# Two interleaved attention and squared-ReLU layers on one core: sums and biases off GpSimd, output bias written into the accumulator banks, own buffers for the first token pair, the full chunk first

## The chip, the cores and the metric

One core of a Trainium2 chip runs the whole program. The metric is the device time of one execution in microseconds (us); of several runs the median counts.

## The reference

Two layers, each a linear attention block (A) and a dense block (B), on 2048 tokens of 640 columns in float32:

```
x = x + A(layernorm(x));  x = x + B(layernorm(x));  and both once more, with the same weights
A: q, k, v = x @ wqkv  (32 heads of 20);  phi(t) = where(t > 0, t + 1, exp(t)) + 1e-6
   kv = sum over tokens of phi(k) (x) v;  z = sum over tokens of phi(k)
   o = phi(q) @ kv / (phi(q) . z + 1e-6);  A = o @ wo
B: h = relu(x @ w1 + b1);  B = (h * h) @ w2 + b2      (w1: 640 x 1728, w2: 1728 x 640)
```

## The kernel before

The 2048 tokens are 16 tiles of 128 (`t`), and four tiles make a group of 512 tokens (`g`). Each float32 operand of a matmul is split into a high part, rounded to the format fp32r, and a low part, the rest: a copy on ScalarE makes the high part, a subtraction on VectorE the low part, and a product is three matmuls (high x low, low x high, high x high).

Each layer has two stages. The **attention stage** goes over the 16 tiles with an order written out by hand. It makes `phi(k)` and `phi(q)`, stores `phi(q)` in DRAM (`pqd`), and sums up the products from which `kv` is made; `phi(q)` of some tiles is made late, at the end of the stage (`late_q`), and the last such piece within the next stage (`late_line`). In layer 0 the stage also splits the weights of B and keeps the halves in DRAM (`Prep`, lines 409 to 475); pairs of 128-row chunks of w1 are turned into the four sums and differences of a Strassen scheme (`Prep.sums`, four additions on GpSimd). Then `kv` and `wo` are multiplied into one matrix M, and tiles 0 to 3 get the attention output and become x1.

The **second stage** is ordered by a planner that runs while the program is built: `Clock` (line 80 on) keeps a time for each engine, and a set of generators (`Line`s, each with a rank; the lower goes first) give their next step with an estimated cost. `Clock.run` puts TensorE's steps one after the other and fills the other engines' queues up to TensorE's time. The instructions stand in each engine's queue in the order in which the planner took them, and every engine works its queue in order. A step may be of kind `"any"`: then the planner puts it on the engine that ends it first. The lines are:

- `fc1_line`: the first layer of B, for each group 14 chunks of hidden units. `STEPS` gives their order: chunk 13 (64 units, both halves of its weights side by side in one matmul, 10 matmuls), chunk 12 (15 matmuls), then six Strassen steps of two chunks each (`Strassen.seg1` to `seg5`, matmuls at line 1497 and 1507). Chunk 12 goes into bank `h`, chunk 13 into bank `h1`; the Strassen steps use both.
- `act` (line 1576): what follows each chunk. For a full chunk: ReLU with bias on ScalarE (line 1585), the square rounded on ScalarE (1598), the square in full on VectorE or GpSimd (1599), the low part on VectorE (1588). For chunk 13 five shorter steps (1618, 1604, 1608, 1591, 1592).
- `fc2_line`: the second layer of B. For each chunk, in the order in which they were made, its product with w2 (`fc2_tile`, line 1646) is added into five banks: `a0` to `a3`, one for each tile with 512 output columns, and `as`, the other 128 columns turned, for all four tiles. The first chunk of a group (`FIRST` = 13) starts the sums in a bank, and after the last (`LAST` = 11) VectorE adds the bank to x1 (`tile_add`, line 1695; the turned strip goes by block moves, line 1672).
- For tiles 4 to 15, in pairs: `q_line` loads and turns `phi(q)` (line 766) and splits it (`p_split`); `pair_line` makes the sums of the Strassen scheme (`s_turns`, line 1747, VectorE or GpSimd), splits them into `so`, and does seven products (`Pair`, matmuls at line 567, all into bank `po0`, additions at line 1813); `x_line` does the layer norm, turns the tile (lines 542 to 555) and splits it into the group's buffer `xTb`, and then `bias` adds b2 to x1 on GpSimd (`f_bias`, line 835) and stores it. `t_line` makes the first-layer sums (`t_sums`, line 1337) and splits them into `tx`. A pair's `q_line` starts when the pair before is turned (`("turned", t - 2)`), and its split waits for the products of the pair before (`("p", ...)`).
- `bias_line` does the same `bias` for tiles 0 to 3; `late_line` the last late `phi(q)`; `ring_line` loads B's weights into a ring of buffers in the order of `uses` (line 367; the load is at line 496), each as soon as a buffer is free. All loads and stores of this stage go through SyncE's queue, in order.

Of the kernel before, what the change touches and what calls it, by code (L numbers as in the profile page):

```python
# [13 lines left out]
P = 128  # L14
# [3 lines left out]
DC = D // P  # L18
# [22 lines left out]
STEPS = (("p", 13), ("p", 12), *(("w", i) for i in range(NW)))  # L41
FIRST, LAST = 13, 11
# [37 lines left out]
class Clock:  # L80
# [22 lines left out]
    def head(self, line):  # L103


        while not line.over:
# [26 lines left out]
            elif h[0] == "end f":  # L133
                self.f += [line.got - HOP if len(h) > 2 else line.ready - HOP] * h[1]
# [91 lines left out]
def kernel(  # L226
# [39 lines left out]
    b2bc = cpool.tile([P, D], F32, name="b2bc")  # L266
    b1sb = cpool.tile([P, NF], F32, name="b1sb")
# [100 lines left out]
    for g in range(NG):  # L368
        for kind, c in STEPS:
# [4 lines left out]
            else:  # L374
                q = (13, 12) if c == 0 else (2 * c - 2, 2 * c - 1)
# [33 lines left out]
    class Prep:  # L409


        def __init__(self):
# [7 lines left out]
            self.pair, self.summed = {}, set()  # L420
# [19 lines left out]
        def sums(self, c):  # L440

            r0, r1 = self.pair[c]
# [9 lines left out]
        def high(self):  # L452
            if self.raws:
                nm, c, raw = self.raws.pop(0)
                while nm in ("wG", "wH") and c not in self.summed:
                    self.low()
                u = utile("uprep")[:, : unit_len(nm, c)]
# [164 lines left out]
    for layer in range(N_LAYERS):  # L622
# [209 lines left out]
        def f_bias(t):  # L832

            v = xr.pop(t)
            nc.gpsimd.tensor_tensor(out=v, in0=v, in1=b2bc, op=ALU.add)
            yield
            nc.sync.dma_start(x1d[t], v)

# [52 lines left out]
        for t in range(NT):  # L891
# [173 lines left out]
            for _ in range(4):  # L1065
                prep.low()
            if gt and not is_late:
# [257 lines left out]
        def t_sums(t, eng):  # L1325
# [5 lines left out]
            for out, x, y in (  # L1331
# [5 lines left out]
                eng[0].tensor_tensor(out=out, in0=x, in1=y, op=ALU.subtract)  # L1337
# [42 lines left out]
        for i in (2, 3):  # L1380
# [10 lines left out]
        list(t_sums(0, [nc.gpsimd]))  # L1391
# [5 lines left out]
        list(t_sums(2, [nc.vector]))  # L1397
# [4 lines left out]
        ta, tb, so = wtile("uT13"), wtile("uT42"), wtile("uS")  # L1402
        ta, tb, so = (
            ta.rearrange("p (j m n) -> p j m n", j=2, m=2),
            tb.rearrange("p (j m n) -> p j m n", j=2, m=2),
            so.rearrange("p (j n) -> p j n", j=2),
# [30 lines left out]
        x1_first, pT_first = [x1_tile()], [pT_tile()]  # L1437

# [9 lines left out]
        def fc1(g, c):  # L1448
            ps = fresh("h" if c == 12 else "h1")
# [101 lines left out]
        def both(cols, f):  # L1551
            eng = {"DVE": nc.vector, "POOL": nc.gpsimd}
            return "any", [(e, cost(e, cols)) for e in eng], lambda e: f(eng[e])

# [3 lines left out]
        def stepped(it, eng, cols):  # L1558
            def f(e):
                eng[0] = e  # L1560
                next(it)

            return both(cols, f)

        slots = {"h": [0.0] * 3, "hr": [0.0] * 3}

# [9 lines left out]
        def act(c, ps, at):  # L1576
# [19 lines left out]
            def full():  # L1596
                yield "ready", there
                yield "ACT", cost("ACT", GT), lambda: nc.scalar.activation(h[:, 0], r, AF.Square)  # L1598
                yield both(GT, lambda e: e.tensor_tensor(out=r, in0=r, in1=r, op=ALU.mult))  # L1599
# [3 lines left out]
            def half():  # L1603
# [3 lines left out]
                free[1] = line.ready  # L1607
# [9 lines left out]
            else:  # L1617
                at = ck.chain("ACT", cost("ACT", GT), lambda: nc.scalar.activation(
                    r[:FL], ps[FL:], AF.Identity, bias=b1sb[FL:, 13:14]
                ), at)  # L1620
                line = ck.add(half(), 0, at)
# [4 lines left out]
        def fc2_tile(g, c, h, i, s=slice(0, DM), new=False):  # L1626
# [3 lines left out]
            first, last = c == FIRST, c == LAST  # L1630
# [4 lines left out]
            ps = accs[g, i]  # L1635
            if i < TG:
# [8 lines left out]
            for k, (l, r) in enumerate(a):  # L1645
                nc.tensor.matmul(  # L1646
                    ps, l, r, start=(first or new) and k == 0, stop=end and k == len(a) - 1
                )

# [85 lines left out]
        def s_turns(t, eng):  # L1735


            z0, z1 = yzp.pop(t), yzp.pop(t + 1)
            a, b, r = slice(0, 2 * P), slice(2 * P, 4 * P), slice(4 * P, D)
            for out, x, y, op in (  # L1740
# [6 lines left out]
                eng[0].tensor_tensor(out=out, in0=x, in1=y, op=op)  # L1747
# [9 lines left out]
        def p_split(t, first=0):  # L1757

            u = pT_first.pop() if pT_first else pT_tile()
# [19 lines left out]
        class Pair:  # L1779
# [21 lines left out]
            def turned(self, c):  # L1801
# [466 lines left out]
```

## Time and profile before

| | |
|---|---|
| median of 3 runs | 1389.21 us (1384.1 to 1390.07) |
| the profiled execution | 1390.24 us, span 1388.4 us |
| TensorE busy | 1337.4 us, 96% |
| VectorE / ScalarE / GpSimd busy | 1014.8 / 744.8 / 235.1 us |
| mean granted TensorE clock | 0.990 |
| additions of b2 on GpSimd | 32, 54.2 us |

In the rows a line begins with the line of the code, the engine (PE is TensorE, DVE VectorE, ACT ScalarE, POOL GpSimd, SPq SyncE's queue of DMA issues), the operation, and what it writes and reads with its shape. In a timeline the first two numbers are start and length in us, and a bracket gives the idle time before and what ended it. In a wait row three numbers follow: us in total, how often, the longest. Groups have a count, then busy us and mean ns. A row of stretches has the stretch, its length, busy us and instructions of the five engines, the granted clock, the DMA engines' busy share and GB/s. The attention stage of layer 0 ends at about 260 us, layer 1's second stage begins at about 947 us.

### The profile page before, as it was taken

What the parts mean: (1) busy time and instruction counts of PE and PEld (TensorE: products, weight loads), DVE (VectorE), ACT (ScalarE), POOL (GpSimd) and SP (SyncE); (2) the same over time, 40 slices, a digit from 0 to 9 for tenths busy, and PEclk for the clock granted to TensorE, in tenths of its full rate; (3) what the DMA queues carried; (4) which work ended last, traced back from release to release, by engine and by line L of the source; (5) the groups of instructions that cost most, each with busy time, mean ns of one, the idle gap of its engine ahead of it and who ended that gap; (6) DMA issues with size and microseconds to landing.
All of it is one profiled execution on the core that took longest, in us unless ns stands there. A gap on an engine that the chain in (4) does not pass through costs nothing.

```text
span 1388.4 us, 21426 instructions
## 1 busy us (share of the span) xinstructions
PE 1337.4 (96%) x7616; PEld 1184.3 (85%) x7616; DVE 1014.8 (73%) x1883; ACT 744.8 (54%) x1724; POOL 235.1 (17%) x264
## 2 busy tenths in 40 slices
PE   9999999889989999999999999998999999999999
PEld 8888889778877988988888889997887888888887
DVE  8888968879768778755256778788788877875323
ACT  5888845635545444536436777564255445454321
POOL 2334310301102001100012232103012111020000
PEclk9999999999999999999999999999999999999999
DMA  6678686397787688699741114264976977687685
GB/s 199 223 267 328 246 273 191 124 320 248 243 258 248 235 264 294 216 366 346 259 155 57 58 39 122 53 200 161 354 245 213 308 243 261 203 291 268 235 316 175
DMA packets 120096, 316.10 MB, mean 228 GB/s; under 512 B 14966, under 2 KB 40182, under 8 KB 119318
## 3 DMA queue, kind: packets, MB, share of 16 engines
q1 hardware_dynamic: 118478, 312.06, 66.1%
q10 hardware_dynamic: 1512, 2.69, 0.7%
q8 instruction: 60, 0.98, 0.3%
q14 instruction: 46, 0.38, 0.1%
HBM read 251.28 MB, written 64.85 MB: 228 GB/s over the span
## 4 chain that ended last, share of the span: by engine, by line
PE 55%; DVE 19%; DMA 13%; ACT 5%; issue 3%; SPq 3%; POOL 1%; ACTq 0%; DVEq 0%; POOLq 0%
PE PS L567 21%; PE PS L1646 17%; PE PS L1497 12%; DMA pqt<-pq 5%; PE PS L1507 3%; ACT z L555 2%; DMA u<-kept_w 2%; SPq L766 1%; DMA u<-kept_wH 1%; PE PS L1463 1%; DVE e L678 1%; DMA u<-kept_wF 1%; DVE bn L517 1%; DVE z L553 1%; DVE uprep L404 1%
## 5 line engine op out<-in xcount | busy, mean ns | idle before, releaser
L1646 PE MATMUL PS<-u,h 128*128 128x512 f32 x1318 | 342.0, 395 | 8.9 <-DVE h L1592 6.5
L555 ACT ACTIVATE z<-y 32x160 f32<-32x160 f32 x781 | 261.1, 334 | 57.8 <-DVE y L542 37.6
L1646 PEld LDWEIGHTS PS<-u,h 128*128 128x128 f32 x1318 | 242.6, 191 | 55.6 <-DVE h L1592 7.3
L567 PE MATMUL PS<-kq,xT 128*128 128x320 f32 (+2 forms) x1575 | 283.6, 335 | 2.5 <-DVE r L679 2.2
L567 PEld LDWEIGHTS PS<-kq,xT 128*128 128x128 f32 x1575 | 251.3, 189 | 28.5 <-DVE r L679 2.5
L1497 PE MATMUL PS<-tx,u 128*128 128x256 f32 x1152 | 162.7, 284 | 8.5 <-DMA u<-kept_wH 3.7
L1585 ACT ACTIVATE hr<-PS,b1sb 128x512 f32<-128x512 f32 x104 | 71.3, 686 | 173.6 <-PE PS L1507 156.8
L1497 PEld LDWEIGHTS PS<-tx,u 128*128 128x128 f32 x1152 | 150.7, 192 | 15.2 <-ACT s L1519 5.2
L1497 PEld LDWEIGHTS PS<-xTb,u 128*128 128x128 f32 x864 | 120.9, 192 | 24.6 <-DVE PS L1539 6.8
L1497 PE MATMUL PS<-xTb,u 128*128 128x256 f32 x864 | 129.4, 286 | 9.8 <-DVE PS L1539 4.4
L567 PE MATMUL PS<-kh,xh 128*128 128x512 f32 x480 | 126.8, 398 | 0.0
L1599 DVE TENSOR_TENSOR hr<-hr 128x512 f32<-128x512 f32 x98 | 68.0, 700 | 76.9 <-ACT h L1598 76.5
L522 POOL TENSOR_SCALAR rs<-mv 128x1 f32<-128x1 f32 x62 | 29.1, 470 | 544.4 <-DVE mv L519 537.8
L567 PEld LDWEIGHTS PS<-kh,xh 128*128 128x128 f32 x480 | 88.9, 192 | 15.2
L1598 ACT ACTIVATE h<-hr 128x512 fp32r<-128x512 f32 x104 | 64.6, 628 | 61.9 <-PE PS L1646 60.4
L670 ACT ACTIVATE e<-PS 128x320 f32<-128x320 f32 (+4 forms) x128 | 53.2, 434 | 81.8 <-PE PS L567 68.6
L1646 PE MATMUL PS<-h,u 128*128 128x512 f32 x328 | 92.6, 391 | 0.0
L678 DVE TENSOR_SCALAR e<-e 128x320 f32<-128x320 f32 (+4 forms) x128 | 49.7, 388 | 47.6 <-ACT e L670 46.9
L1588 DVE TENSOR_TENSOR h<-hr,h 128x512 fp32r<-128x512 f32 x104 | 75.9, 735 | 3.4
L854 POOL TENSOR_TENSOR acc<-acc,r 128x640 f32<-128x640 f32 x28 | 51.2, 1829 | 156.5 <-DVE r L679 156.5
L1507 PE MATMUL PS<-xTb,u 128*128 128x512 f32 x288 | 76.8, 393 | 0.0
L1646 PEld LDWEIGHTS PS<-h,u 128*128 128x128 f32 x328 | 59.9, 188 | 11.0
(173 smaller groups left out, 1949.5 us busy)
## 6 DMA issues: line engine op xcount, KB each, us to landing
u<-kept_w SPq DMA_DIRECT2D x116, 640.0 KB, 5.8
u<-kept_wE SPq DMA_DIRECT2D x48, 512.0 KB, 4.9
u<-kept_wH SPq DMA_DIRECT2D x48, 512.0 KB, 5.5
u<-kept_wG SPq DMA_DIRECT2D x48, 512.0 KB, 5.4
u<-kept_wF SPq DMA_DIRECT2D x48, 512.0 KB, 5.7
x<-x SPq DMA_DIRECT2D x48, 320.0 KB, 6.0
pqt<-pq SPq DMA_DIRECT2D x128, 80.0 KB, 5.8
x<-xr SPq DMA_DIRECT2D x32, 320.0 KB, 6.3
```

The lines of the kernel that those rows point to most:

```text
L555: nc.scalar.activation(d, v, AF.Copy)
L567: nc.tensor.matmul(ps, a, b, start=first and i == 0, stop=last and i == 2)
L670: nc.scalar.activation(self.e[:, a:b], ps, AF.Exp)
L678: nc.vector.tensor_scalar(e, e, 1.0, PHI_EPS, op0=ALU.min, op1=ALU.add)
L854: nc.gpsimd.tensor_tensor(out=acc, in0=acc, in1=r, op=ALU.add)
L1497: nc.tensor.matmul(ps, l[:, d], r[:, d], start=start and d == 0 and n == 0, stop=d == 1 and n == 2, skip_group_check=True,)
L1507: nc.tensor.matmul(ps, l[:, k], r, start=False, stop=n == 2, skip_group_check=True)
L1585: nc.scalar.activation(r, ps, AF.Relu, bias=b1sb[:, c : c + 1])
L1588: nc.vector.tensor_tensor(out=h[:, 1], in0=r, in1=h[:, 0].bitcast(F32), op=ALU.subtract)
L1598: yield "ACT", cost("ACT", GT), lambda: nc.scalar.activation(h[:, 0], r, AF.Square)
L1599: yield both(GT, lambda e: e.tensor_tensor(out=r, in0=r, in1=r, op=ALU.mult))
L1646: nc.tensor.matmul(ps, l, r, start=(first or new) and k == 0, stop=end and k == len(a) - 1)
```

## The change

- **Full chunk first.** In group 0 of each layer chunk 12 goes ahead of chunk 13, and chunk 13 is put into bank `po0` there. The order of the weight loads follows. In the other groups the order stays, and a Strassen step waits in the plan until chunk 13's bank is read.
- **Sums.** `s_turns` and `t_sums` are on VectorE alone. The full square of a chunk may go to VectorE or ScalarE. `Prep.sums` stays on GpSimd but is issued later, behind the tile's other GpSimd work.
- **Output bias.** For tiles 0 to 3 the addition of b2 to x1 goes from GpSimd to VectorE. For groups 1 to 3 it is gone: ScalarE writes b2 into each accumulator bank (`preset`) after the bank has been read, and the group's first matmul adds to it; x1 is stored as soon as it is there (`x1_keep`). A second copy of b2's last 128 values, one per partition, is loaded for that.
- **Own buffers.** The first pair (tiles 4 and 5) keeps its split operands in the buffer that group 1's `xTb` takes later (`early`). The second pair's `q_line` starts after the first pair's `q_line`, and waits no longer for the first pair's products; `x_line` of group 1 waits until the first pair is done.
- `late_line` goes from rank 4 to 1, and the first sums of group 0 wait for it in the plan.

The diff, cut; the names behind `#` say where a line stands.

```diff
-STEPS = (("p", 13), ("p", 12), *(("w", i) for i in range(NW)))
-FIRST, LAST = 13, 11
+UNITS = tuple(("w", i) for i in range(NW))
+STEPS = ((("p", 12), ("p", 13), *UNITS), *(NG - 1) * ((("p", 13), ("p", 12), *UNITS),))
+LAST = 11
...
+        nc.sync.dma_start(b2col, b2[DM:].rearrange("(p o) -> p o", o=1))
...
-                q = (13, 12) if c == 0 else (2 * c - 2, 2 * c - 1)
+                q = (12, 13) if (g, c) == (0, 0) else (13, 12) if c == 0 else (2 * c - 2, 2 * c - 1)
...
                 if nm == "wF":
-                    self.sums(c)
-                    self.summed.add(c)
+                    self.to_sum = c
...
-            nc.gpsimd.tensor_tensor(out=v, in0=v, in1=b2bc, op=ALU.add)
+            nc.vector.tensor_tensor(out=v, in0=v, in1=b2bc, op=ALU.add)
...
+        def x1_keep(t):
+            nc.sync.dma_start(x1d[t], xr[t])
...
             for _ in range(4):
                 prep.low()
+            prep.sums()
...
-                eng[0].tensor_tensor(out=out, in0=x, in1=y, op=ALU.subtract)      # t_sums
+                nc.vector.tensor_tensor(out=out, in0=x, in1=y, op=ALU.subtract)
...
+        early = tmp.tile([P, 2 * DC * GT], R32, tag="T", name="early", bufs=2)
+        so_of = {TG: early[:, 4 * D : 6 * D + 8 * P].rearrange("p (j n) -> p j n", j=2)}
...
-            ps = fresh("h" if c == 12 else "h1")
+            ps = fresh("h" if c == 12 else "h1" if g else "po0")
...
+            def square(e):
+                if e == "ACT":
+                    nc.scalar.activation(r, r, AF.Square)
+                else:
+                    nc.vector.tensor_tensor(out=r, in0=r, in1=r, op=ALU.mult)
...
-                yield both(GT, lambda e: e.tensor_tensor(out=r, in0=r, in1=r, op=ALU.mult))
+                yield "any", [(e, cost(e, GT)) for e in ("DVE", "ACT")], square
...
+        def preset(g, i):
+            accs[g, i] = ps = fresh(f"a{i}" if i < TG else "as")
+            if i < TG:
+                nc.scalar.activation(ps, b2bc[:, :DM], AF.Copy)
+            else:
+                nc.scalar.activation(ps, b2col.to_broadcast([P, GT]), AF.Copy)
...
-                eng[0].tensor_tensor(out=out, in0=x, in1=y, op=op)                 # s_turns
+                nc.vector.tensor_tensor(out=out, in0=x, in1=y, op=op)
...
-            u = pT_first.pop() if pT_first else pT_tile()                          # p_split
+            if t < TG + 2:
+                k = t - TG
+                u = early[:, 2 * k * D : 2 * (k + 1) * D].rearrange("p (j n) -> p j n", j=2)
+            else:
+                u = pT_first.pop() if pT_first else pT_tile()
...
-            yield "need", ("p", (t - 2) // 2 * 2)                                  # q_line
+            if t > TG + 3:
+                yield "need", ("p", (t - 2) // 2 * 2)
...
+            yield "need", ("p", t - 2)                                             # pair_line, after the turns
...
+            yield "SP", MB, store                                                  # x_line: x1_keep
...
-            yield "need", ("group", t // TG - 1)                                   # x_line
+            yield "need", ("group", t // TG - 1), ("p", TG)
...
-            yield from bias(t)                                                     # end of x_line
...
+                    yield "until", lambda: not half_of                             # fc1_line, before seg1
...
+                        if g < NG - 1:
+                            ck.add(preset_line(g + 1, i), 2, free["a", i])         # after tile_add
...
-            after = ("turned", t - 2)
+            after = ("q", t - 1) if t == TG + 2 else ("turned", t - 2)
...
-        ck.add(late_line(), 4, 7.5)
+        ck.add(late_line(), 1, 7.5)
```

More of the change, by code (lines that the diff above doesn't have):

```diff
@@ L1629, in fc2_tile @@
             wh, wl = u[:, :D], u[:, D:]
-            first, last = c == FIRST, c == LAST
+            first, last = (g, i) not in accs, c == LAST
             end = last or last_layer and (g, i, c) == (NG - 1, TG - 1, 9)
@@ L1646, in fc2_tile @@
                 nc.tensor.matmul(
[L1647 removed]
+                    ps, l, r, start=(first or new) and k == 0, stop=end and k == len(a) - 1, **loose
                 )
+        def preset(g, i):
[4 more added lines that the diff above has]
+                nc.scalar.activation(ps, b2col.to_broadcast([P, GT]), AF.Copy)
         strips = {}
@@ L1871 @@
         ck.t["ACT"], ck.t["DVE"] = 4.5, 4.8
-        free = {0: 0.0, 1: 0.0, **{("a", i): 0.0 for i in range(TG + 1)}}
+        free = {0: 0.0, 1: 0.0, 2: 0.0, **{("a", i): 0.0 for i in range(TG + 1)}}
         done = ck.done
@@ L1981, in bias @@
             it = f_bias(t)
-            yield "POOL", cost("POOL", D), lambda: next(it)
+            yield "DVE", cost("DVE", D), lambda: next(it)
             def store():
@@ L2138, in fc1_line @@
                         yield "until", room
-                        turned(g, c, fresh("h1" if k else "h"), k)
+                        turned(g, c, fresh(("h", "h1", "po0")[k]), k)
                         continue
@@ L2168, in fc1_line, with preset_line, f @@
                     turned(g, 2 * c + 1, st.h1, 1)
+        def preset_line(g, i):
+            line = ck.lines[-1]
+            def f():
+                preset(g, i)
+            yield "ACT", cost("ACT", DM), f
+            free["a", i] = line.ready
         def fc2_line():
```

79 lines of the change are left out of this document (46 added, 33 removed).

## The prediction

> **What bounds the kernel now.** I read the page's busy times first, then the waits of TensorE, then the timeline where those waits lie, then the clock there.
>
> ```profile
> span 1388.4 us, 21426 instructions
> PE 1337.4 (96%) x7616; PEld 1184.3 (85%) x7616; DVE 1014.8 (73%) x1883; ACT 744.8 (54%) x1724; POOL 235.1 (17%) x264
> ...
> PE PS L567 <- DVE xr L1813: 7.9, 6, 2.8
> PE PS L1646 <- DVE h L1592: 6.5, 3, 3.5
> ...
> PE PS L1463 <- DVE xTb L1777: 3.7, 2, 2.2
> ```
>
> TensorE works in all but 51.0 us (1388.4 - 1337.4), and the change takes no matmul away. So whatever it brings must come out of those 51.0 us, or out of the time that matmuls lose to a lowered clock. A wait row gives the total, the number of times and the longest: a few long waits, nearly all on VectorE. The three on L1592 (the low half of hidden chunk 13, the 64-row chunk with which each group opens) are 1.49 us at the start of each layer's group 0 and 3.52 us at layer 0's step from group 0 to 1. Layer 0's group 0 starts so:
>
> ```profile
> 261.81 5.96 PE L1463 MATMUL PS<-xTb,u 128*128 128x512 f32 x25 [0.63 <-ACT xTb L283]
> ...
> 268.76 0.98 PE L1497 MATMUL PS<-xTb,u 128*128 128x256 f32 x6 [0.99 <-DVE hr L1604]
> ...
> 272.79 7.18 POOL L835 TENSOR_TENSOR xr<-xr,b2bc 128x640 f32<-128x640 f32 x4
> 273.07 1.57 DVE L1591 CAST h<-hr 64x512 fp32r<-64x512 f32 x1
> ...
> 274.68 1.92 DVE L1592 TENSOR_TENSOR h<-hr,h 64x512 fp32r<-64x512 f32 x1
> ...
> 276.65 1.19 PE L1646 MATMUL PS<-u,h 128*128 128x512 f32 x4 [1.49 <-DVE h L1592]
> ...
> 278.95 0.98 PE L1497 MATMUL PS<-xTb,u 128*128 128x256 f32 x6 [1.11 <-DVE PS L1539]
> ...
> 280.70 0.32 SPq L2087 DMA_DIRECT2D pq<-rl  x1
> ...
> 283.81 0.38 SPq L496 DMA_DIRECT2D u<-kept_wH  x1
> ...
> 288.59 0.98 PE L1497 MATMUL PS<-tx,u 128*128 128x256 f32 x6 [1.80 <-DMA u<-kept_wH]
> ...
> 290.17 4.47 PE L1646 MATMUL PS<-u,h 128*128 128x512 f32 x12 [0.60 <-DMA u<-kept_w]
> ```
>
> Four bias additions hold GpSimd from 272.79 to 279.97, and in that time VectorE's steps for chunk 13 take 1.57 and 1.92 us; at the next group, beside no bias, the same two take 0.41 and 0.69 (rows below). So TensorE waits 1.49 and 1.11 us there. The 0.99 us before are for bank h1, which chunk 13 and the first product of the Strassen steps share. The two waits for weights follow from SyncE's queue: the load of wH stands at 283.81 behind the store of the late `phi(q)` row, issued at 280.70.
>
> ```profile
> 288.00:292.00 4.00, 2.81 (x10) 2.27 (x11) 3.90 (x8) 2.09 (x5) 0.00 (x0) 0.74 1.00 372
> 292.00:296.00 4.00, 4.00 (x19) 3.15 (x18) 0.90 (x3) 0.71 (x2) 0.00 (x0) 0.84 1.03 419
> ...
> 394.00:398.00 4.00, 2.94 (x10) 2.46 (x11) 3.93 (x8) 1.80 (x5) 0.00 (x0) 0.71 0.11 46
> 398.00:402.00 4.00, 4.00 (x24) 3.72 (x24) 1.81 (x6) 0.75 (x2) 0.00 (x0) 0.86 0.81 306
> ...
> 972.00:980.00 8.00, 5.76 (x21) 4.62 (x22) 5.79 (x11) 2.43 (x5) 0.00 (x0) 0.79 1.02 386
> ```
>
> The third column from the right is the granted clock. After the waits it falls: 4 x 0.26 + 4 x 0.16 = 1.68 us lost at 288 to 296, 4 x 0.29 + 4 x 0.14 = 1.72 at 394 to 402, 8 x 0.21 = 1.68 in layer 1. These are counted as busy, so waits cost more than the idle time says.
>
> **The change, part by part.** *Start of group 0 (full chunk first, chunk 13 in bank po0, biases and late row).* Chunk 12 now goes first and chunk 13 into a bank of its own, so the 0.99 us go. The four biases move to VectorE, where each is one 640-column addition, 0.81 us by the row of L1813 below, four 3.2 us in all; they are queued at rank 6, behind the hidden chunks, so I cost them at nothing. Without that cover they cost TensorE the 1.11 us that it waits for VectorE now. The 1.49 and 1.11 us go. Sum: 0.99 + 1.49 + 1.11 = 3.59 us a layer. The waits for weights (1.80 + 0.60 = 2.40) and the lost clock (1.68) go if the late row is stored before it blocks SyncE, for which the change raises its rank. But the DMA engines are full there (shares 1.00 and 1.03), so I count half: (2.40 + 1.68) / 2 = 2.04. Against this stands a new wait: the weights of w2 chunk 12 go to the buffer that the first chunk's 15 matmuls free.
>
> ```profile
> u<-kept_w SPq DMA_DIRECT2D x116, 640.0 KB, 5.8
> ```
>
> They end at 261.81 + 5.96 x 15/25 = 265.4, and a load lands 5.8 us later, at 271.2. TensorE could use it from about 269.5 (25 matmuls, then the first products). The planner in the code reckons a landing of 3.7 us (1.3 + 0.655/0.39 + 0.7), so it may place this work 2.1 us too early: between 0 and 2.1, I take 1.5, since its error is one-sided. Net: 3.59 + 2.04 - 1.5 = 4.1 a layer, 8.3 for two.
>
> *Group 0 to group 1 (own buffers for the first token pair).*
>
> ```profile
> 300.80 1.85 SPq L766 DMA_DIRECT2D pqt<-pq  x4
> ...
> 324.13 0.49 DVE L1813 TENSOR_TENSOR xr<-PS,xr 128x320 f32<-128x320 f32 x1
> ...
> 337.65 1.04 PE L567 MATMUL PS<-uM,pT 128*128 128x320 f32 x6
> ...
> 385.58 5.96 PE L1463 MATMUL PS<-xTb,u 128*128 128x512 f32 x25 [1.52 <-DVE xTb L1777]
> ...
> 393.87 0.41 DVE L1591 CAST h<-hr 64x512 fp32r<-64x512 f32 x1
> 394.32 0.69 DVE L1592 TENSOR_TENSOR h<-hr,h 64x512 fp32r<-64x512 f32 x1
> ...
> 395.06 2.41 PE L1646 MATMUL PS<-u,h 128*128 128x512 f32 x6 [3.52 <-DVE h L1592]
> ...
> 1065.49 5.96 PE L1463 MATMUL PS<-xTb,u 128*128 128x512 f32 x25 [2.20 <-DVE xTb L1777]
> ```
>
> Group 1 starts late because its tokens are late: tile 6's `phi(q)` is loaded only when tiles 4 and 5 are turned (300.80), its split waits for the first pair's last product (324.13), so the second pair starts at 337.65, 13.5 us after the first ended. Meanwhile group 0's work runs out, and nothing is left to lay beside the opening of group 1. With its own buffers the first pair holds up nobody: the second pair is loaded after `("q", 5)` and may start when the first ends. A lead of up to 13.5 us covers the 1.52 us, and group 0's remaining second-layer products then cover the 3.52. With the clock 1.52 + 3.52 + 1.72 = 6.76 in layer 0 and 2.20 in layer 1: 8.96. VectorE, the only other thing on that chain, may keep part of it: three quarters, 6.7.
>
> *The rest of VectorE's load.*
>
> ```profile
> 240.00:560.00 320.00, 298.82 (x1720) 265.23 (x1719) 254.04 (x461) 159.61 (x367) 50.25 (x57) 0.98 0.75 251
> ...
> L835 POOL TENSOR_TENSOR xr<-xr,b2bc 128x640 f32<-128x640 f32 x32 | 54.2, 1708 | 1.7 <-DVE xn L532 1.7
> ...
> L1747 POOL TENSOR_TENSOR z<-z 128x256 f32<-128x256 f32 (+1 forms) x16 | 13.5, 846 | 81.2 <-DVE z L1747 27.0 <-DMA u<-kept_w 16.9 <-DVE z L798 14.9
> ...
> L1747 DVE TENSOR_TENSOR z<-z 128x256 f32<-128x256 f32 (+1 forms) x44 | 19.0, 439 | 2.1 <-POOL z L1747 1.3
> ...
> L1813 DVE TENSOR_TENSOR xr<-su,xr 128x640 f32<-128x640 f32 x12 | 9.7, 811 | 0.0
> ...
> L1598 ACT ACTIVATE h<-hr 128x512 fp32r<-128x512 f32 x104 | 64.6, 628 | 61.9 <-PE PS L1646 60.4
> L1599 DVE TENSOR_TENSOR hr<-hr 128x512 f32<-128x512 f32 x98 | 68.0, 700 | 76.9 <-ACT h L1598 76.5
> ```
>
> VectorE is busy 79% of 240 to 560 (254.04 of 320). It takes over 16 turns at 0.44 us (7.0), about as many first-layer sums (under 7 at the same price), and 8 biases at 0.81 (6.5): some 20 us. It is freed of 32 biases beside it: by the pairs 1.57 against 0.41 and 1.92 against 0.69, one bias costs VectorE about 1.2 us where it is busy, so up to 38 us. And the second square of a hidden chunk, 0.70 us on VectorE, may now run on ScalarE for 0.63 (104 chunks; ScalarE stands at 54%). On balance VectorE gets lighter, by 18 us without the squares. The 7.9 us that TensorE waits on L1813 are VectorE's lateness: I count 3 of them (bounds: -3, if the sums stand ahead of the pair's additions, to 7.9).
>
> *Output bias in the banks.* For groups 1 to 3 of each layer ScalarE writes the bias into five accumulators, 30 writes of 512 columns. No such write is in the trace; the nearest rows are 0.63 us (L1598, the same size) and, at the low end, nothing, if TensorE has Strassen products to run in between. Each write stands between the addition that empties a bank and the next group's first matmul on it. In six steps between groups one write of the five can be late: 0 to 6 x 0.63 = 3.8; I take 2.
>
> *At nothing.* The weight sums of the preparation stay on GpSimd and only go behind the tile's running sum and statistics; who waits is the split of wG and wH on ScalarE, a tile later in the common order; without that cover, four sums of about 1 us on ScalarE's path once per pair. One more 512-byte constant load stands in SyncE's queue ahead of the first-layer bias, 0.4 us of issue, covered by the whole attention stage. The 24 stores of x1 leave earlier, as many as before.
>
> Sum: 8.3 + 6.7 + 3 - 2 = 16.0 us. The profiled execution took 1390.24 us (span 1388.4), so 1374.2; it lies 1.03 above the median 1389.21, so 1373.2: I say **1373 us**.
>
> One rule speaks against the clock's share. The Trainium skill, page "TensorE: Matmul & The Clock Gate", Part 1, says that the clock halves only after an idle window of about 3.4 us. By it, removing waits of 1.8 and 0.6 us wins no clock, and the sum would lack 2 x 0.84 + 1.3 = 3.0 us: 1376. The rows above disagree: clock 0.74 right after waits of 1.80 and 0.60 us.
>
> **Rivals.** *The preset becomes the wait (slower).* ScalarE works in order, and at a step between groups it moves blocks:
>
> ```profile
> 376.24 4.14 ACT L555 ACTIVATE z<-y 32x160 f32<-32x160 f32 x12
> ```
>
> A preset behind such a run holds the next group's accumulator by 4.14 + 0.63 = 4.8 us. If TensorE has nothing else, at all six steps, that is 28.6 us in place of my 2: 1373 - 2 + 28.6 = 1400. It decides from 18 / 6 = 3.0 us a step on. For it: no step has more than ScalarE's spare 46% to hide in. Against: the planner gives presets rank 2, ahead of block moves. 13%.
>
> *The weights take the start back (no change).* The DMA share of 1.00 to 1.04 after 288 lets nothing arrive sooner; an earlier start waits longer. The 8.3 us go, and half of the 6.7: 1373 + 8.3 + 3.4 = 1385. For it: the full slices; against: the next slices are not full, and SyncE's blocked queue explains the two waits. 13%.
>
> *It doesn't speed up the pairs.* VectorE, not the buffers, sets their pace; the 20 us that come to it are on the path and the relief falls elsewhere. Then 8.3 and -2 stay, 6.7 and 3 go, and 10 of the 20 us are paid: 1389 - 6.3 + 10 = 1393. For it: 79% busy; against: the 13.5 us between the pairs are a named buffer wait. 7%, half of it within 0.5%.
>
> **How the numbers follow.** 0.5%, 7 us, is about what a measurement of this kernel can tell from no change: faster means below 1382. The forecast has 67%: its own range is 1360 to 1382, from all of the 2 x 7.67 and 8.96 us with some of the 7.9 down to 7 us. Within 0.5%: 13% + 4% = 17%. Slower: 13% + 3% = 16%. The range leaves out the upper part of the slow cases and the best few per cent: 1359 to 1392.
>
> **What would show it.** Right: no bias rows on GpSimd; no wait of L1646 on L1592 at group 0; the second pair's first product within 4 us of the first pair's last addition; group 1 without a wait on xTb; the slices at 0.74 and 0.71 back near 1.00. Wrong: TensorE waiting for the presets' ScalarE rows or for u<-kept_w near the start of group 0; VectorE busier than 79%; new waits of L567 on L1813 above 7.9 us.

## The result and the profile after

The changed kernel takes 1379.54 us (median of 9 runs, 1374.84 to 1382.9) against 1386.26 us for the kernel before beside it (9 runs, 1380.48 to 1390.07): a ratio of **0.9949, 95% interval 0.9935 to 0.9964**. That is 7 us less, where 16 were forecast. The profiled execution of the changed kernel took 1382.9 us, its span is 1381.2 us, its mean granted clock 0.994.

The page's busy times after:

```profile
span 1381.2 us, 21322 instructions
PE 1337.4 (97%) x7616; PEld 1180.7 (85%) x7616; DVE 982.9 (71%) x1928; ACT 770.5 (56%) x1753; POOL 147.2 (11%) x196
```

TensorE's busy time is to the tenth what it was, 1337.4 us; its idle time fell from 51.0 to 43.8 us, and these 7.2 us are the whole difference of these two spans (two other traces, below, split theirs otherwise). VectorE got lighter by 31.9 us (1014.8 - 982.9), though 8 biases and all the sums came to it; 18.6 of these are 27 squares that it gave up (71 of 104 are left on it, 98 before, 0.69 us each; ScalarE has 33, 6 of them from GpSimd). The waits of TensorE after:

```profile
PE PS L1510 <- DMA u<-kept_wH: 5.9, 3, 2.3
PE PS L574 <- DVE r L686: 5.8, 2, 3.5
PE PS L574 <- DVE uu L1839: 5.1, 5, 2.4
PE PS L1510 <- DVE PS L1552: 4.6, 6, 1.5
PE PS L574 <- DVE xr L1839: 4.5, 6, 1.5
PE PS L1510 <- DMA u<-kept_wG: 3.7, 4, 1.2
```

The old waits on the low half of chunk 13 (6.5 us) and on group 1's tokens (3.7 us) are not in the list any more. In their place stand waits for weights (wH 5.9 and wG 3.7, before 3.7 and 1.3; with wE and the halves of w2, `kept_w`, 10.3 in all, before 8.0) and for the pairs' additions (line 1839, before 1813: 5.1 + 4.5, before 7.9). SyncE's queue at the start of layer 0's group 0 shows what stands before the load of the third Strassen step's wH:

```profile
284.38 7.60 SPq L773 DMA_DIRECT2D pqt<-pq  x8
292.08 0.38 SPq L503 DMA_DIRECT2D u<-kept_w  x1
292.56 0.38 SPq L503 DMA_DIRECT2D u<-kept_wE  x1
292.99 2.15 SPq L1752 DMA_DIRECT2D x<-x  x4
295.24 0.46 SPq L503 DMA_DIRECT2D u<-kept_wH  x1
```

TensorE's timeline and its clock there:

```profile
261.83 5.95 PE L1476 MATMUL PS<-xTb,u 128*128 128x512 f32 x25 [0.83 <-ACT xTb L286]
...
274.39 0.97 PE L1510 MATMUL PS<-xTb,u 128*128 128x256 f32 x6 [0.53 <-DVE PS L1552]
...
276.59 2.96 PE L1659 MATMUL PS<-u,h 128*128 128x512 f32 x12
...
288.62 0.95 PE L1510 MATMUL PS<-tx,u 128*128 128x256 f32 x6 [1.16 <-DMA u<-kept_wG]
...
302.97 0.98 PE L1510 MATMUL PS<-tx,u 128*128 128x256 f32 x6 [1.87 <-DMA u<-kept_wH]
```

```profile
288.00:292.00 4.00, 2.86 (x16) 2.69 (x17) 2.62 (x6) 1.63 (x3) 0.00 (x0) 0.79 0.96 275
292.00:296.00 4.00, 3.48 (x19) 3.19 (x19) 3.14 (x7) 0.74 (x1) 0.00 (x0) 0.78 0.81 268
...
304.00:308.00 4.00, 4.00 (x15) 3.47 (x14) 2.18 (x4) 1.50 (x4) 0.00 (x0) 0.57 1.01 414
...
398.00:402.00 4.00, 4.00 (x30) 3.73 (x29) 3.52 (x7) 3.76 (x10) 0.00 (x0) 1.00 0.34 95
```

The first product with w2 starts at 276.59, as before (276.65). At the step to group 1 the clock is back at 1.00 (before 0.71 and 0.86), but at the start of group 0 it is no better than before. Where the 7.2 us lie is seen in the second stages, cut at the first matmul of group 0, of group 1, and at the turned strip that ends the stage. Before, and then after:

```profile
261.81:385.58 123.77, 112.68 (x627) 98.11 (x627) 99.32 (x174) 61.30 (x138) 22.06 (x21) 0.97 0.78 265
385.58:706.60 321.02, 310.37 (x1770) 273.87 (x1771) 209.56 (x389) 149.41 (x344) 28.65 (x39) 0.99 0.79 274
...
946.94:1065.49 118.55, 108.05 (x611) 93.83 (x611) 95.02 (x168) 55.52 (x123) 21.45 (x21) 0.99 0.79 265
1065.49:1380.90 315.41, 308.69 (x1772) 270.98 (x1772) 197.46 (x362) 137.58 (x309) 32.64 (x36) 1.00 0.74 255
```

```profile
261.83:379.42 117.59, 110.14 (x621) 96.77 (x622) 97.43 (x190) 64.01 (x135) 4.43 (x8) 0.97 0.77 267
379.42:699.30 319.88, 313.43 (x1777) 273.85 (x1776) 193.22 (x383) 161.97 (x366) 11.63 (x25) 0.99 0.79 277
...
940.90:1055.22 114.32, 106.90 (x609) 93.24 (x609) 94.91 (x185) 61.29 (x132) 3.96 (x8) 0.99 0.78 269
1055.22:1373.70 318.48, 310.52 (x1776) 271.32 (x1774) 185.22 (x370) 142.27 (x310) 7.31 (x16) 1.00 0.73 253
```

Length minus TensorE's busy time is its idle time: 11.1, 10.6, 10.5 and 6.7 us before, 7.5, 6.4, 7.4 and 8.0 after. The two groups 0 won 3.6 and 3.1 us and the rest of layer 0 4.2; the rest of layer 1 lost 1.2, and 2.5 were lost outside these stretches, 2.3 of them in layer 0's attention stage.

### The profile page after: what moved, and what is told of

It is laid out like the page before. It is cut to its first block, busy times and chain, and to the rows that moved or that the text cites. A ratio compares the mean times of both kernels' runs of the same rounds, so it can differ in the third digit from the quotient of the medians.

```text
span 1381.2 us, 21322 instructions
## 1 busy us (share of the span) xinstructions
PE 1337.4 (97%) x7616; PEld 1180.7 (85%) x7616; DVE 982.9 (71%) x1928; ACT 770.5 (56%) x1753; POOL 147.2 (11%) x196
## 4 chain that ended last, share of the span: by engine, by line
PE 71%; DMA 12%; DVE 11%; issue 2%; SPq 2%; ACT 1%; POOL 1%; ACTq 0%; DVEq 0%; POOLq 0%
PE PS L574 25%; PE PS L1659 21%; PE PS L1510 15%; PE PS L1520 4%; DMA pqt<-pq 4%; DMA u<-kept_wH 2%; PE PS L1476 2%; DMA u<-kept_w 2%; DMA u<-kept_wG 1%; SPq L773 1%; DMA u<-kept_wE 1%; PE PS L1188 1%; DVE bn L524 1%; DVE uprep L407 1%; PE PS L927 1%
## 5 line engine op out<-in xcount | busy, mean ns | idle before, releaser
L1659 PE MATMUL PS<-u,h 128*128 128x512 f32 x1318 | 346.1, 397 | 1.4 <-ACT s L1532 0.7
L562 ACT ACTIVATE z<-y 32x160 f32<-32x160 f32 x767 | 256.1, 334 | 88.4 <-DVE y L549 69.3
L1510 PE MATMUL PS<-tx,u 128*128 128x256 f32 x1152 | 162.7, 284 | 11.1 <-DMA u<-kept_wH 5.9
L1594 DVE TENSOR_TENSOR hr<-hr 128x512 f32<-128x512 f32 x71 | 48.7, 687 | 73.6 <-ACT h L1607 73.3
L1597 DVE TENSOR_TENSOR h<-hr,h 128x512 fp32r<-128x512 f32 x104 | 70.9, 685 | 11.4 <-ACT hr L1592 7.4
L685 DVE TENSOR_SCALAR e<-e 128x320 f32<-128x320 f32 (+4 forms) x128 | 41.5, 325 | 50.8 <-ACT e L677 50.3
```

What stands on the lines that cost most here:

```text
L562: nc.scalar.activation(d, v, AF.Copy)
L685: nc.vector.tensor_scalar(e, e, 1.0, PHI_EPS, op0=ALU.min, op1=ALU.add)
L1510: nc.tensor.matmul(ps, l[:, d], r[:, d], start=start and d == 0 and n == 0, stop=d == 1 and n == 2, skip_group_check=True,)
L1594: nc.vector.tensor_tensor(out=r, in0=r, in1=r, op=ALU.mult)
L1597: nc.vector.tensor_tensor(out=h[:, 1], in0=r, in1=h[:, 0].bitcast(F32), op=ALU.subtract)
L1659: nc.tensor.matmul(ps, l, r, start=(first or new) and k == 0, stop=end and k == len(a) - 1, **loose)
```

## The experiments

All ratios are against the kernel before, run beside; the intervals are 95%.

**Is it an address?** The new constant `b2col` shifts every later buffer by 32 bytes, and most of the second-layer matmuls (1306 of 1646, the group `PS<-u,h`) take 398 ns on average after, 396 before. One kernel gives the old code that shift, the other takes it from the new code.

```diff
 # e1, in the kernel before
-    scalars = cpool.tile([P, 2], F32, name="scalars")
+    scalars = cpool.tile([P, 10], F32, name="scalars")
 # e2, in the changed kernel
-    b2col = cpool.tile([P, 1], F32, name="b2col")
+    b2col = scalars[:, 2:3]        # scalars made [P, 3]
```

> The kernel before with one constant tile made 32 bytes longer and nothing else, so that every buffer behind it on that side of SBUF starts 32 bytes later, as the new constant of the change does. The second layer's 1646 matmuls then read one operand at 0 and the other at 32 modulo 64 bytes, where both were at 32. Theory address: they take about 4 ns longer each, 1646 x 0.0035 = 5.5 us; their group goes from 342.0 towards 346 us busy, the time to 0.4% above the kernel before, the waits stay. Rival order: the slower matmuls of the changed kernel come from its order or its accumulation into written banks; then this kernel keeps 342 us and the time of before within 0.15%. Rival chance: the pace differs from execution to execution; then the time is that of before and the busy sum is anywhere from 342 to 346.

> The changed kernel with its new bias column in the unused room of a constant tile, so that no buffer moves against the kernel before. Theory address: the second layer's matmuls go back from 346.1 to about 342 us busy, and the time to 0.4% below the changed kernel: ratio to the kernel before 0.991 (1374 us), faster than both. Rivals order and chance: 346 us stays, or comes and goes, and the ratio is 0.995 as for the changed kernel.

Measured: e1 0.9986 (0.9966 to 1.0005), e2 0.9964 (0.9944 to 0.9983). The smaller group of these matmuls, in e1 and in e2 (391 ns before, 395 after):

```profile
L1646 PE MATMUL PS<-h,u 128*128 128x512 f32 x328 | 93.8, 395 | 0.0
```

```profile
L1659 PE MATMUL PS<-h,u 128*128 128x512 f32 x328 | 92.8, 391 | 0.0
```

The pace of this group follows the address (395 ns with the shift, 391 without, in both codes); in the large group the medians do (394 and 389), while its busy time doesn't show the theory's 346 against 342 us: 342.8 in e1, 342.0 in e2. The time doesn't follow either: e1 isn't slower than the kernel before, and e2 lies far from the 0.991 of the theory. As the cause of the missing 9 us the address falls.

The two kernels serve for one thing more. e1 has as many instructions on every engine as the kernel before, e2 as the changed one: they are second traces of the same two plans, with buffers moved by 32 bytes. Idle in the four stretches named above is 11.0, 9.0, 8.5 and 3.8 us in e1 and 9.3, 7.6, 8.1 and 8.3 in e2. One plan thus differs by up to 2.9 us in a stretch from trace to trace, and from e1 to e2 the idle time hardly falls (45.7 to 45.5 us) while the busy time does (1338.4 to 1333.0). Three things stand in both pairs of traces: the waits at the step to group 1 go, the waits for weights at the start of group 0 rise (both layers together 4.7 and 2.7 us before and in e1, 6.3 and 7.3 after and in e2), and the rest of layer 1 loses.

**The biases.** e6 puts the four biases of group 0 back on GpSimd and leaves the rest of the change; e15 does the opposite, the kernel before with all its 32 biases on VectorE and no other edit.

```diff
 # e6, in the changed kernel; e15 the other way round in the kernel before
-nc.vector.tensor_tensor(out=v, in0=v, in1=b2bc, op=ALU.add)
+nc.gpsimd.tensor_tensor(out=v, in0=v, in1=b2bc, op=ALU.add)
-yield "DVE", cost("DVE", D), lambda: next(it)
+yield "POOL", cost("POOL", D), lambda: next(it)
```

> The changed kernel with the four biases of group 0 back on GpSimd. Theory contention: where they run, VectorE's steps of 512 columns take 1.6 to 1.9 us in place of 0.4 to 0.7, and the product of the first chunk with w2 and the sums of the Strassen step come 1 to 2.6 us later in each layer: ratio to the kernel before 0.996 to 0.999 (2 to 5 us slower than the changed kernel). Rival, the new order has slack there (the first chunk's product waits for nothing): within 1 us of the changed kernel, ratio 0.994 to 0.996.

> The kernel before with one thing altered: its 32 bias additions run on VectorE (0.82 us each, 26 us more for it) in place of GpSimd (1.7 us each). Theory (GpSimd's additions slow VectorE beside them, by the forecast 1.2 us each, up to 38 us; putting the four of group 0 back cost the changed kernel 8 us): 5 to 9 us below the kernel before, ratio 0.9935 to 0.9965. Rival (26 us more on the engine that TensorE waits for eat up what is freed): ratio 0.998 to 1.004.

Measured: e6 1.0009 (0.9989 to 1.0029), some 8 us above the changed kernel. That is more than the theory's 2 to 5 us, and it lies elsewhere: in this plan the four biases run ahead of group 0, not beside its first chunks. e6's timeline of GpSimd and VectorE just ahead of group 0:

```profile
253.73 7.04 POOL L842 TENSOR_TENSOR xr<-xr,b2bc 128x640 f32<-128x640 f32 x4
253.80 1.86 DVE L539 TENSOR_SCALAR xn<-xr,mv,rs 128x640 f32<-128x640 f32 x1 [0.77 <-POOL rs L530]
255.59 1.68 DVE L685 TENSOR_SCALAR e<-e 128x320 f32<-128x320 f32 x1
257.30 0.49 DVE L686 SCALAR_TENSOR_TENSOR rl<-PS,e 128x320 f32<-128x320 f32 x1
257.71 1.67 DVE L287 TENSOR_TENSOR xTb<-z,xTb 128x640 fp32r<-128x640 f32 x1
```

The same steps in the changed kernel, without the biases beside them:

```profile
256.06 0.62 DVE L539 TENSOR_SCALAR xn<-xr,mv,rs 128x640 f32<-128x640 f32 x1 [0.77 <-POOL rs L530]
256.59 0.32 DVE L685 TENSOR_SCALAR e<-e 128x320 f32<-128x320 f32 x1
256.95 0.49 DVE L686 SCALAR_TENSOR_TENSOR rl<-PS,e 128x320 f32<-128x320 f32 x1
257.36 0.82 DVE L287 TENSOR_TENSOR xTb<-z,xTb 128x640 fp32r<-128x640 f32 x1
```

Beside GpSimd's additions 0.62 becomes 1.86, 0.32 becomes 1.68, 0.82 becomes 1.67; the step that reads a matmul bank (0.49) doesn't change. So xTb is late, and TensorE waits 11.3 us for it at group 0 of the two layers (1.7 in the changed kernel):

```profile
PE PS L1476 <- ACT xTb L286: 11.3, 2, 5.6
```

The Trainium skill, page "SBUF — State Buffer", section "SBUF: two separate sides", gives this a form: a port pair shared by VectorE and GpSimd is an exclusive lock, and the loser stands still for a whole instruction. The rows agree: each of the three lengthened steps ends 0.02 to 0.4 us after one of the four additions does (7.04 / 4 = 1.76 us each).

e15 came out at 1.0096 (1.0071 to 1.0122), 13 us slower, and both expectations are missed. VectorE is relieved here too: busy 1003.0 us against 1014.8, though it took 32 x 0.82 = 26 us more (16 steps, some 7 us, went from it to GpSimd in this plan). But TensorE now waits 15.9 us for group 1's tokens, before 3.7:

```profile
PE PS L1463 <- DVE xTb L1777: 15.9, 2, 9.8
```

So a lighter VectorE isn't yet a faster kernel: in this plan its work for group 1 is done later.

**Chunk 12 first.** e5 undoes this part alone; chunk 13 keeps its own bank.

```diff
-STEPS = ((("p", 12), ("p", 13), *UNITS), *(NG - 1) * ((("p", 13), ("p", 12), *UNITS),))
+STEPS = NG * ((("p", 13), ("p", 12), *UNITS),)
-q = (12, 13) if (g, c) == (0, 0) else (13, 12) if c == 0 else (2 * c - 2, 2 * c - 1)
+q = (13, 12) if c == 0 else (2 * c - 2, 2 * c - 1)
```

> The changed kernel with chunk 13 first in group 0 again, still in a bank of its own. Theory: with the bank of its own and the biases off GpSimd the order is worth little, since the late row of phi(q) holds back every second-layer product until about 276 us; ratio 0.994 to 0.997. Rival, the full chunk first is what took the wait on L1592 away: the wait comes back with 1.5 us a layer and the ratio is 0.997 to 0.999.

Measured: 1370.27 us, 0.9879 (0.9846 to 0.9911). Both expectations are missed: without this part the kernel is 9 us faster. Its clock and its groups, cut as above:

```profile
261.07:373.21 112.14, 105.71 (x605) 91.70 (x606) 90.43 (x180) 60.27 (x125) 3.75 (x8) 1.00 0.80 273
373.21:692.90 319.69, 314.92 (x1793) 275.77 (x1792) 196.31 (x389) 168.14 (x379) 11.23 (x25) 0.99 0.79 279
...
935.13:1041.58 106.45, 102.22 (x590) 88.87 (x591) 85.95 (x171) 58.24 (x123) 3.74 (x8) 1.00 0.79 274
1041.58:1360.10 318.52, 314.41 (x1792) 274.15 (x1791) 192.18 (x385) 146.45 (x316) 7.61 (x16) 1.00 0.74 257
```

Idle 6.4, 4.8, 4.2 and 4.1 us, against 7.5, 6.4, 7.4 and 8.0: 9.8 us less in all, spread over the stages. TensorE's busy time is 2.5 us less too (1334.9); the clock of layer 0's group 0, 1.00 in place of 0.97, would give 117.59 x 0.03 = 3.5. Yet the waits for weights at layer 0's start are nearly as long as in the changed kernel, 1.77 + 0.79 against 1.16 + 1.87 us (in layer 1 they are shorter, 0.68 + 0.72 against 0.24 + 0.79 + 2.25):

```profile
282.95 0.98 PE L1510 MATMUL PS<-tx,u 128*128 128x256 f32 x6 [1.77 <-DMA u<-kept_wH]
...
286.11 3.06 PE L1659 MATMUL PS<-u,h 128*128 128x512 f32 x12 [0.79 <-DMA u<-kept_w]
```

```profile
284.00:288.00 4.00, 3.21 (x14) 2.31 (x13) 3.27 (x5) 2.40 (x5) 0.00 (x0) 1.00 1.04 417
288.00:292.00 4.00, 4.00 (x28) 3.48 (x27) 1.58 (x4) 1.01 (x2) 0.00 (x0) 1.00 1.02 356
```

**Own buffers and early loads.** e3 only lets the second pair's loads wait for the first pair again, e4 undoes the own buffers too (and with them the plan's condition for starting these loads, which the change had lowered from five free temporary buffers to four); e9 and e10 are e3 and e4 with chunk 13 first.

```diff
 # e3, e9
-            after = ("q", t - 1) if t == TG + 2 else ("turned", t - 2)
+            after = ("turned", t - 2)
 # e4, e10 besides
-            if t > TG + 3:
-                yield "need", ("p", (t - 2) // 2 * 2)
+            yield "need", ("p", (t - 2) // 2 * 2)
 ...          # early gone: pT and so come from the shared buffers
```

> The changed kernel, but the second token pair's phi(q) loads again wait until the first pair is turned; the first pair keeps its own buffers. Theory (queue): in the changed kernel the second pair's eight loads stand in SyncE's queue in one run of 7.6 us (284.38 to 292.0 in layer 0, 963.50 in layer 1) ahead of the weights wE and wH, and the waits of TensorE for wH (1.87 and 2.25 us) with the lowered clock behind them are their price. Then the run of eight is gone, the two waits fall below 0.7 us, the time is 4 to 6 us below the changed kernel, a ratio of 0.991 to 0.992 against the kernel before. Rival (order): the loads are no matter, and what costs at the start of group 0 is that chunk 12 goes ahead of chunk 13; then the ratio stays at 0.994 to 0.996. Second rival (lead): the early loads are what gave group 1 its start; then the waits at group 1's start (1.52 and 2.20 us) come back with a lowered clock and the ratio is 0.998 to 1.000.

> The changed kernel without own buffers for the first token pair: its transposed rows take the shared buffers as before, and the second pair's loads wait until the first is turned. Theory (the forecast's 6.7 us for this part): the waits of TensorE at the step from group 0 to group 1 come back (3.5 + 1.5 us with the clock in layer 0, 2.2 us in layer 1), the time is 6 to 8 us above the changed kernel, ratio 0.999 to 1.001 against the kernel before. Rival (the biases alone gave the 7 us that were gained, as the run with the biases back on GpSimd suggests): ratio 0.993 to 0.997, the same as the changed kernel within 2 us.

> The changed kernel with chunk 13 ahead of chunk 12 in group 0 again (which alone gave a ratio of 0.988) and with the second pair's loads late, own buffers kept. Theory (queue): late loads help here as they do with chunk 12 first, by 2 to 4 us, ratio 0.985 to 0.987. Rival (order): with chunk 13 first the loads already come four and four, behind the weights, so nothing is left to win; the second pair's lead is lost instead, ratio 0.988 to 0.992.

> The changed kernel with chunk 13 ahead of chunk 12 in group 0, and without own buffers for the first token pair (with chunk 12 first, the same without own buffers gave 1.007). What is left of the change: sums and biases off GpSimd, bias written into the accumulators, chunk 13's bank of its own. Theory (chunk 12 first is the costly part, in every setting): at least 9 us below the kernel without own buffers, ratio 0.990 to 0.997, and the waits at group 1's start are back at 2 us or less. Rival (the two parts only hurt or help together: own buffers are what matters, the order costs only beside the early loads): ratio 1.000 to 1.007, with waits at group 1's start of 4 us or more.

Measured: e3 0.999 (0.9974 to 1.0007), e4 1.0072 (1.0043 to 1.0101), e9 0.986 (0.9837 to 0.9883), e10 0.9978 (0.9961 to 0.9994). In e3 the waits for wH at the start of both layers' group 0 are gone, as the queue theory said, but in layer 0 TensorE waits 8.0 us for group 1's tokens instead, and the time is that of the second rival, which had named 1.52 and 2.20 us. e9 lies where the queue theory put it, but can't be told from e5. e4 misses both expectations; its first wait row:

```profile
PE PS L1475 <- DVE xTb L1797: 16.5, 2, 8.8
```

Without own buffers the time rises by 17 us with chunk 12 first (e4) and by 14 with chunk 13 first (e10), in both cases with long waits at group 1's start (16.5 and 9.3 us). With own buffers and late loads but chunk 13 first (e9, 1366.41 us) the kernel is the fastest of all, with 1.5 us of that wait. So e10's expectations each hold by half: the time is 13 us better than e4's, but the waits remain, and the ratio lies between the two ranges.

**The bias writes.** e7 adds b2 to x1 on VectorE for groups 1 to 3 and leaves out the 30 writes of ScalarE.

```diff
-                            ck.add(preset_line(g + 1, i), 2, free["a", i])
 ...
+            yield from bias(t)         # at the end of x_line
```

> The changed kernel without the bias writes into the accumulators: the output bias of groups 1 to 3 is added to x1 on VectorE (24 additions of 0.82 us, 19.7 us more for VectorE), and ScalarE's 30 writes of 0.6 us are gone. Theory (presets cost nothing, as the traces show 0.3 us of waits on them): the only effect is VectorE's 19.7 us; if a third of them reaches TensorE, as in the 71% busy engine's waits, the time is 4 to 8 us above the changed kernel, ratio 0.998 to 1.001. Rival (the forecast's term: presets cost 2 us and VectorE has room): the time is 1 to 3 us below the changed kernel, ratio 0.993 to 0.994.

Measured: 0.9957 (0.993 to 0.9984), between the two expectations, and not to be told from the changed kernel. Its plan is another one, with 7.1 us of waits for group 1's tokens.

**How much is the plan?** One number of the planner is altered, and no work is added or taken away: in the changed kernel (e13) and in e9 (e14). With the plan, some steps change their engine too (ScalarE has 28 instructions more in e13, VectorE 28 fewer).

```diff
-"DVE": (0.08, 1.04e-3)
+"DVE": (0.1, 1.04e-3)
```

> The changed kernel with one number of its planner altered: a step of VectorE is reckoned at 0.10 us fixed in place of 0.08. No instruction is added or taken away, no buffer moves, but the order is planned anew. Theory (the parts have prices of their own): the order is about as good, the time within 2 us of the changed kernel, ratio 0.993 to 0.997. Rival (chance of the plan): any edit shuffles the whole order of the layer, and that alone is worth several us; then the time is more than 4 us off, below 0.992 or above 0.998, and prices of parts below 5 us cannot be read from single edits of this kernel.

> The same altered number in the best kernel so far (chunk 13 ahead of chunk 12, own buffers, second pair's loads late; ratio 0.986). Theory (the parts have prices of their own, chunk 13 first is worth about 9 us and more): ratio 0.984 to 0.988, and still at least 0.006 below the changed kernel with the same altered number. Rival (chance of the plan): the lead of this kernel goes, ratio 0.990 or more.

Measured: e13 0.9999 (0.9978 to 1.0019), e14 0.996 (0.9938 to 0.9982). The rival holds in both: the same work under another plan costs 7 us in the one and 14 in the other, as much as the change gained or more, and e14 is only 0.0039 below e13 where 0.006 were asked. Both are the same alteration and both cost time, so this is one sample of what a plan can do; whether other plans win as often as they lose isn't shown. In both the wait for group 1's tokens is there again; e14's first wait row:

```profile
PE PS L1476 <- DVE xTb L1802: 9.9, 2, 6.3
```

Side by side, with TensorE's wait for xTb at group 1's start (both layers) and its whole idle time (span minus busy):

| kernel | ratio | wait, group 1 | idle |
|---|---|---|---|
| before | 1 | 3.7 | 51.0 |
| e1 before, 32 bytes | 0.9986 | 3.1 | 45.7 |
| changed | 0.9949 | 0 | 43.8 |
| e2 changed, not shifted | 0.9964 | 0 | 45.5 |
| e5 13 first | 0.9879 | 0 | 32.7 |
| e9 13 first, late loads | 0.986 | 1.5 | 33.3 |
| e14 e9 replanned | 0.996 | 9.9 | 46.2 |
| e7 no bias writes | 0.9957 | 7.1 | 40.3 |
| e10 13 first, no own buffers | 0.9978 | 9.3 | 48.8 |
| e3 late loads | 0.999 | 8.0 | 45.1 |
| e13 replanned | 0.9999 | 6.2 | 46.3 |
| e6 biases on GpSimd | 1.0009 | 0 (group 0: 11.3) | 50.6 |
| e4 no own buffers | 1.0072 | 16.5 | 54.0 |
| e15 before, biases on VectorE | 1.0096 | 15.9 | 62.4 |

The three fastest kernels start group 1 nearly without a wait, the two slowest wait longest. In between the wait says little: e14 waits 9.9 us and e2 not at all, at the same ratio. Chunk 13 first was faster than chunk 12 first each time the two were put against each other: by 9.7 us (changed to e5), 18 (e3 to e9), 13 (e4 to e10) and 5 (e13 to e14, which differ in the loads too). Own buffers were faster by 11 (e4 to e3) and 16 us (e10 to e9), with the early loads by 17 (e4 to changed) and 14 (e10 to e5); all from the ratios, 0.001 being 1.39 us. The signs agree throughout; but as replanning alone moved 7 and 14 us, the sizes are those of these plans, and no single difference of that size or less is shown to be the part's own.

## Why the prediction was right or wrong

The direction was right, by less than half the amount: 1373 forecast, 1379.54 measured, inside the range. Part of that is luck: the forecast started from the 1389.21 us of three runs, while the kernel before took 1386.26 beside the changed one; 0.9949 of 1389.21 is 1382.1, the very end of the forecast's 1360 to 1382. Term by term, in TensorE's idle time of the two traces, the 7.2 us are 7.2 at the step to group 1, 3.0 at the start of group 0, 0.7 in the rest of layer 0, and losses of 1.2 in the rest of layer 1 and 2.5 outside:

- **Group 0 to group 1, forecast 6.7: it held, as far as this plan goes.** The waits of 1.52, 3.52 and 2.20 us are all gone, 7.2 us, and the clock at 398 to 402 is 1.00. Taking the buffers out brings waits of 9.3 and 16.5 us back (e10, e4). That the lead of up to 13.5 us would cover these waits whatever the order was too much: e13 and e7 have buffers and early loads and wait 6.2 and 7.1 us. The second pair starts 332.27 - 326.95 = 5.3 us after the first pair's last addition (326.46 + 0.49 = 326.95); 4 were named.

```profile
326.46 0.49 DVE L1839 TENSOR_TENSOR xr<-PS,xr 128x320 f32<-128x320 f32 x1
```

```profile
332.27 1.05 PE L574 MATMUL PS<-uM,pT 128*128 128x320 f32 x6
```

- **Start of group 0, forecast 8.3: the step that failed.** Up to group 1 the idle time fell by 3.6 + 3.1 = 6.7 us in the two layers, and 1.52 + 2.20 of it are the waits just told: 3.0 are left. The waits of VectorE's making went as named: the 0.99 and the 1.49 are gone, the 1.11 is 0.53; the 1.5 us reckoned against them didn't come, as the first product with w2 (276.59) waits for nothing. But the half of the waits for weights and of the clock that was to go, 2.04 us a layer, did not: in layer 0 1.80 and 0.60 became 1.16 and 1.87, in layer 1 1.70 and 0.61 became 0.24, 0.79 and 2.25, and at 288 to 296 and 304 to 308 the clock lost 4 x (0.21 + 0.22 + 0.43) = 3.4 us, where 1.68 were lost before. The late row no longer blocks SyncE, and the second Strassen step's wH, issued at 275.39 and no longer at 283.81, comes in time. Its wG doesn't: issued at 280.56, it lets TensorE go on only at 288.62, beside full DMA engines (0.96 to 1.03). And TensorE, 3.7 us further ahead by the third step (300.23 against 303.91), waits for that step's wH, whose load stands behind eight loads of the second pair that hold the queue for 7.6 us. Tile 6's stood at 300.80 before: a DMA that the change moved past the weights, and that the forecast costed nowhere. That this is not the whole of it e3 shows: with these loads late the wait for wH goes and the time still rises. And that chunk 12 ahead is worth 3.6 us a layer rested on waits that the other parts remove as well: e5 has chunk 13 first, no wait on chunk 13's low half either, and is 9 us faster. The reason within the plan isn't settled: e5's lead is spread over all four stretches.
- **The rest of VectorE's load, forecast 3: wrong sign.** VectorE did get lighter, by 31.9 - 18.6 = 13 us without the squares where 18 were reckoned, but TensorE's waits on the pairs' additions grew from 7.9 to 9.6 us (in the second traces from 6.4 in e1 to 8.4 in e2). The opening reading, that the waits are nearly all on VectorE, holds for the rows shown there; of all 47 us of waits in the trace before, VectorE has 31 and the weights 8.
- **Bias writes, forecast -2: next to nothing.** No matmul waits on them in the changed kernel; one weight load does, for 0.8 us. In other traces matmuls wait up to 1.9 us on them (e9), far from the 4.8 a step of the rival that saw them as the next wait, which falls. e7 has the same time without them, but under another plan, so that it shows no price of theirs.
- **The rival of the weights** (1385) had a mechanism that took back a part of the start's gain, but not the other half of its price: the step to group 1 kept all its gain. The rival of the pairs falls.
- **The clock rule.** After 1.87 us of waiting the clock was 0.57, but in e5 it stayed at 1.00 after waits of 1.77 and 0.79. Nor does the plan alone decide it: in e1, the plan of the kernel before, TensorE waits 1.52 and 0.54 us where it waited 1.80 and 0.60 before, and from 288 to 296 the clock is 1.00 in place of 0.74 and 0.84. So a clock loss behind a wait is neither sure nor excluded, and the sum, which took each loss as bound to the wait before it, was too plain. The Trainium skill, page "TensorE: Matmul & The Clock Gate", Part 1, says that the window over which activity is judged runs free, so that a transition hangs on where in the window the work falls; that fits these cases, while its whole idle window of about 3.4 us was in none of these waits.

What the forecast lacked as a whole is that it treated the plan as fixed. It added up waits removed from one order, while an edit of a rank, a cost or a condition can give another order with waits of its own, worth 7 and 14 us in the two cases tried. It also read each wait from one trace, where a second trace of the same plan differs by up to 2.9 us in a stretch.

## What to carry to other kernels

Where a planner or a scheduler orders the work, measure first what an edit that changes nothing but its numbers does to the time; parts worth less than that can't be told by single edits, and trying some plans may win more than the parts do (e9 against e14: 14 us with the same work). When a condition is loosened so that loads go earlier, list what they now stand ahead of in the queue. And take two traces of a plan before its waits are added up: here the kernel before has 51.0 us of idle time, and e1, its plan with the buffers 32 bytes on, 45.7.

## What was not expected of the hardware

The same matmul, 128x512 with operands moved by 32 bytes, took 395 ns in place of 391 on average, in both codes (e1 and e2), without effect on the time. Beside GpSimd additions of 640 columns VectorE steps ended only about when an addition did, 1.68 us in place of 0.32, while the steps that read a matmul bank kept their 0.49. Nearly equal waits of TensorE for weights, 1.87 and 1.77 us, left the clock at 0.57 in one plan and at 1.00 in another, and one plan had 0.74 in one trace and 1.00 in another.
